# Banded attention, gated projections and an MLP on one core: other PSUM banks for the attention's outputs and its transposes

## The chip, the cores and the metric

The kernel runs on one core of a Trainium2 chip. The metric is the device time of one execution in microseconds (us). Three timed runs of the kernel before gave 503.07, 503.93 and 504.25 us; the median is 503.93 us.

## What is computed

The program is one chain of three layers on two sequences (B = 2) of 768 positions, all in float32. First comes banded attention with eight heads of 64: a position sees the positions less than `n_local` = 96 before it and the first `n_global` = 8, with a linear bias by distance. Second is a gated layer of four experts, each a causal attention of width 64; each position takes the two experts with the highest gate. Third is a low-rank mixing over positions, followed by an MLP of width 2048 (weights arrive as 64-bit floats).

```python
scores = scale * np.matmul(q, k.transpose(0, 1, 3, 2)) + bias      # layer 1, banded
a = np.exp(scores - scores.max(-1)); a = a / (a.sum(-1) + 1e-09)
attn = np.matmul(a, v)
...
ye = softmax(causal((x @ wq[e]) @ (x @ wk[e]).T)) @ (x @ wv[e]) @ wo[e]   # layer 2
out += mask * w * ye
...
u = x + (x.T @ U @ V).T                                           # layer 3
return u + np.maximum(u @ w_ch1, 0.0) @ w_ch2
```

## The kernel before, in words

**Units.** Layer 1 is cut into 48 units (`a_unit`): for each sequence b, four head pairs j, six row blocks i of 128 positions. A unit goes through all engines. TensorE computes the scores into a score bank S (L223). VectorE adds the bias and finds the row minimum (L240), ScalarE takes the exponential (L244), VectorE the reciprocal of the sum (L248, L249), GpSimd scales the rows (L251). TensorE transposes the scaled rows, two or four blocks of 128x128, into one PSUM bank (L185 in `transpose_out`); ScalarE (L189) or, for each fifth unit, VectorE (L191) copies that bank to SBUF as `pt`. At last TensorE multiplies `pt` with the values into the bank X (L260), called the output products here. Three units share one X tile, a third of the columns each. After the third, ScalarE writes the high part of the tile to `xT` (`hi_act`, L62), and VectorE subtracts it from the tile to make the low part (`lo_dve`, L68). Only then can the next tile in the same bank begin.

**Banks.** PSUM has eight banks in this kernel: T, U, X, `acc`, and two pairs for scores, of which one pair is later given to `acd`. `ps(tag)` looks in the dictionary `rot` for a list of banks that a tag uses in turn; a tag that is not there always has its own bank. Before the change the transposes alternate between T and U, and all output tiles lie in X.

**Stages.** `run` names the stages with `go`, which draws yields from generators in proportion. (1) The 24 units of sequence 0 beside 21 of the 24 steps of W' (`W`), which loads the first MLP weight in pieces, narrows it from 64 bits on ScalarE, GpSimd and VectorE (L77, L79, L80, L81), multiplies it by the output projection on TensorE into `acc` (L474) and splits the product on ScalarE and VectorE. Then the rest of W' and the load of the projection weights. (2) The first projections `C(0)` beside the first six units of sequence 1. (3) The causal attention `D` of sequence 0 beside the other 18 units. Later stages hold the second sequence's projections and the MLP.

**Order.** The order of each engine's instructions is fixed when the program is built: a list scheduler takes those whose inputs it holds ready, by their place in the program and by a model of durations. Each engine then works its list in that order. So a change of banks changes which instruction the scheduler holds ready, and may change all five orders. The dense variant (`run(True)`, behind an `If`) uses the same dictionary and is not executed with these inputs.

Of the kernel before, what the change touches and what calls it, by code (L numbers as in the profile page):

```python
# [19 lines left out]
B, H, S, D = 2, 8, 768, 64  # L20
# [6 lines left out]
R = 32  # L27
# [19 lines left out]
class Body:  # L47
# [615 lines left out]
    def run(self, dense):  # L663
        self.cms = {}
        self.last = None
        self.sb = {"pt": 3, "pr": 6}
        self.fl, self.fmod = 0, FA
        self.psb = {"T": 1, "U": 1, "X": 1, "acc": 1, "acd": 2, "h": 2}
        self.psum = self.open("psum", space=PSUM)
        self.psumT = self.open("psumT", space=PSUM)  # L670
        self.psumR = self.open("psumR", space=PSUM)
        self.psumS = self.open("psumS", space=PSUM)
        self.pp = {"U": self.psumT, "S": self.psumS, "R": self.psumR}
        self.rot = {"T": ["T", "U"], "S": ["S", "R"]}
        const = self.open("const")
        self.small = self.open("small")
        wpp = self.open("wpp")
        zp = self.open("zp")
        self.sA = self.open("sA")
        self.consts(const)  # L680
        self.causal(const)
        stk0 = self.open("stk0", "right")
        wpl = self.open("wpl", "right")
        x1p = self.open("x1p", "right")
        x0p = self.open("x0p", "right")
        self.xT = [[x.tile([P, 4, S], F32R, name=self.uid("xT")) for _ in "hl"] for x in (x0p, x1p)]
        ap = self.open("ap")
        if dense:
            for b in range(B):
                self.A_dense(b, ap)  # L690
            gens = [None, None]
        else:
            self.araw = self.open("araw", bufs=2)
            prep = self.a_prep(0, 0, True)
            pre = next(prep)
            bt = self.open("bt")
            self.band_bias(ap, bt)
            self.close(bt)
            next(prep)
            gens = [self.A(0, pre), lambda: self.A(1, self.pre1)]  # L700

        st0 = self.stacks(stk0)
        self.cv = self.open("cv")
        wtmp = self.open("wtmp")
        W = self.W(wpp, wtmp)
        go(self.tc, (gens[0], 24), (W, 19, 0, 21))
        self.wall_load(wpl)
        go(self.tc, (W, 1))
        self.close(wtmp, self.cv)

        A1 = None if dense else gens[1]()
        self.banks("acd")
        go(self.tc, (self.C(0, st0), 14), (A1, 6, 0, 6))
        self.close(x0p)
        self.soft = self.open("soft0", "right")
        zT = [zp.tile([P, 2, S], F32, tag="zT", name=self.uid("zT"))]
        self.banks("R")
        self.fmod = FD
        go(self.tc, (self.D(0, st0, zT[0], "acc"), 12), (A1, 18))
        self.close(self.soft)  # L720
        if not dense:
            self.close(self.araw)
        self.close(ap, self.sA)

        self.banks("acd")
        self.sb["pr"] = 4
        self.soft = self.open("soft")
        s1p = self.open("s1p")
        yp = self.open("yp")
        self.cv = self.open("cv")  # L730
        mp = self.open("mp")
        yT = [[], []]
        st1 = self.stacks(s1p)
        self.uv_load(yp)

        w2p = None
        w2 = self.w2_load(lambda: [
            ((stk0, "qk0"), (stk0, "qk1")), ((mp, "w2z"), (stk0, "v")), ((w2p, "w2a"), (w2p, "w2b")),
            ((w2p, "w2h"), (w2p, "w2l")), ((s1p, "qk0"), (s1p, "qk1")), ((w2p, "w2x"), (w2p, "w2y"))])
        go(self.tc, (self.Y(0, zT[0], yp, yp, yT[0], "X", "T"), 5, PY), (self.C(1, st1), 14), (w2, 5, 0, 5))  # L740
        self.close(x1p, wpl)
        w2p = self.open("w2p", "right")
        self.wo_load(mp)
        zT.append(zp.tile([P, 2, S], F32, tag="zT", name=self.uid("zT")))
        self.rot.update({"T": ["T"], "h": ["U"]})
        self.fmod = FM
        D1 = self.D(1, st1, zT[1], "X")
        self.op = (mp, "o", 2)
        M0 = chain(self.M(0, 0, yT[0][0], mp, w2), self.M(0, 1, yT[0][1], mp))
        Y1 = self.Y(1, zT[1], yp, yp, yT[1], "X", "T")  # L750
        go(self.tc, (D1, 12, PM), (M0, 24, 0, 24))
        go(self.tc, (Y1, 4, PM, 4), (M0, 10))
        self.close(self.psumS)
        self.psumS = self.open("psumS", space=PSUM)
        self.pp["h"] = self.psumS
        self.rot["h"] = ["U", "h", "h"]
        self.op = (self.soft, "pr", 4)
        go(self.tc, (Y1, 1, PM), (self.M(1, 0, yT[1][0], mp), 17))
        go(self.tc, (self.M(1, 1, yT[1][1], mp), 1))
        self.close(w2p, stk0, mp, self.cv, yp, s1p, self.soft, zp, wpp, self.small, const, self.psumS, self.psumR, self.psumT, self.psum)  # L760
# [10 lines left out]
def chain(*gens):  # L771
    for g in gens:
        yield from g
# [4 lines left out]
def go(tc, *gens):  # L778
    live = [[g[0], g[1], 0, *(tuple(g[2:]) + (0, 1 << 30)[len(g) - 2 :])] for g in gens if g[0] is not None]
    while live:  # L780
        live.sort(key=lambda x: x[2] / x[1])
        g = live[0]
        if g[2] >= g[4]:
            live.pop(0)
            continue
        try:
            if g[3]:
                with tc.high_priority(g[3]):
                    next(g[0])
            else:  # L790
                next(g[0])
            g[2] += 1
        except StopIteration:
            live.pop(0)
# [57 lines left out]
```

## Time and profile before

| | us |
|---|---|
| median of three runs | 503.93 |
| lowest, highest | 503.07, 504.25 |
| the profiled execution's own time | 504.68 |
| its span, first to last instruction | 502.9 |
| TensorE busy in the span | 474.5 |

The span is 1.8 us shorter than the execution's own time. Busy time is summed per engine; a matmul's duration overlaps the next one's, so a busy TensorE may still be waiting in small steps. Stages 1 and 2 are the first 128 us or so of the span.

### The profile page before, as it was taken

The page shows a single profiled execution, that of the slowest core. Times are in us where ns is not written, and L with a number is a line of the kernel's source. Part 1 is how long each engine was busy: PE and PEld are TensorE (multiplying, and loading weights), DVE is VectorE, ACT ScalarE, POOL GpSimd, SP SyncE. Part 2 cuts the span into 40 slices and gives each one's busy share as a digit, 9 for nine tenths or more (in the row PEclk, how much of TensorE's full clock was granted, in tenths as well). Part 3 has the DMA queues.
Part 4 walks back from the last instruction along what each step waited for, and adds up shares of the span by engine and source line. Part 5 has one row for each costly group of instructions (what it writes and reads, how often), then busy time and mean ns, then how long its engine had stood idle before and what let it go on. Part 6 is the DMA issues. An engine that isn't in the chain of part 4 may idle for free.

```text
span 502.9 us, 8239 instructions
## 1 busy us (share of the span) xinstructions
PE 474.5 (94%) x2916; PEld 368.0 (73%) x2916; DVE 245.6 (49%) x811; ACT 216.9 (43%) x581; POOL 115.6 (23%) x210
## 2 busy tenths in 40 slices
PE   5789999999899999899999998999999999999995
PEld 3465767798466567797767775878887888888883
DVE  5787877635776775994863236212322211112111
ACT  6667763521778876644553346222212111111111
POOL 4735555410455451211521011100000000000000
PEclk9999999999999999999999999999999999999998
DMA  8854766245021003440210000100000100010002
GB/s 287 290 170 171 241 206 219 88 109 180 1 72 59 1 3 125 151 143 1 84 44 1 1 0 1 45 21 1 0 1 0 65 0 1 0 63 1 0 1 69
DMA packets 17650, 36.68 MB, mean 73 GB/s; under 512 B 2560, under 2 KB 6400, under 8 KB 17600
## 3 DMA queue, kind: packets, MB, share of 16 engines
q1 hardware_dynamic: 15728, 34.49, 21.0%
q10 hardware_dynamic: 1872, 1.58, 0.9%
q8 instruction: 25, 0.41, 0.3%
q14 instruction: 25, 0.20, 0.1%
HBM read 32.91 MB, written 3.15 MB: 72 GB/s over the span
## 4 chain that ended last, share of the span: by engine, by line
PE 72%; DVE 10%; DMA 6%; ACT 5%; issue 4%; POOL 2%; SPq 0%; POOLq 0%; ACTq 0%; DVEq 0%
PE acd L309 17%; PE acc L309 9%; PE acd L310 8%; PE U L309 6%; PE S L223 5%; DMA cr<-in_w_dram 4%; PE acc L310 4%; PE T L185 4%; PE X L260 3%; PE h L309 3%; PE U L310 3%; PE acc L474 3%; PE U L185 2%; PE acc L417 2%; DVE ct L81 2%
## 5 line engine op out<-in xcount | busy, mean ns | idle before, releaser
L309 PE MATMUL acd<-w,hh 128*128 128x512 f32 x256 | 84.0, 404 | 0.7 <-ACT hh L564 0.7
L565 DVE SCALAR_TENSOR_TENSOR hl<-U,hh 128x384 fp32r<-128x384 f32 x43 | 23.9, 556 | 96.0 <-ACT hh L564 93.2
L564 ACT ACTIVATE hh<-U 128x384 fp32r<-128x384 f32 x43 | 21.1, 490 | 83.3 <-PE U L310 55.2
L244 ACT ACTIVATE pr<-e,nm 128x256 f32<-128x256 f32 (+1 forms) x96 | 46.2, 483 | 22.8 <-DVE nm L240 22.6
L251 POOL TENSOR_SCALAR pr<-pr,rec 128x256 f32<-128x256 f32 (+1 forms) x96 | 45.7, 491 | 40.9 <-ACT pr L244 10.1
L309 PEld LDWEIGHTS acd<-w,hh 128*128 128x128 f32 x256 | 46.0, 188 | 12.1 <-ACT hh L564 2.7
L406 POOL TENSOR_SCALAR pm<-pm,rec 128x128 f32<-128x128 f32 (+5 forms) x48 | 32.5, 690 | 93.8 <-DVE rec L404 59.3
L310 PE MATMUL acd<-w,hl 128*128 128x512 f32 x128 | 50.6, 395 | 0.0
L309 PE MATMUL U<-yT,wph 128*128 128x384 f32 x172 | 45.1, 342 | 0.3 <-DVE hl L565 0.3
L223 PE MATMUL S<-kx,qr 64*128 64x256 f32 (+1 forms) x192 | 34.8, 427 | 7.0 <-ACT qr L214 5.9
L309 PE MATMUL acc<-w,hh 128*128 128x512 f32 x128 | 40.6, 395 | 0.0
L399 ACT ACTIVATE pm<-pm,nm 128x128 f32<-128x128 f32 (+5 forms) x48 | 31.7, 662 | 18.9 <-DVE nm L394 18.2
L189 ACT ACTIVATE pt<-T 128x512 f32<-128x512 f32 (+1 forms) x52 | 27.4, 528 | 24.8 <-PE T L185 24.6
L565 DVE SCALAR_TENSOR_TENSOR hl<-h,hh 128x384 fp32r<-128x384 f32 x21 | 11.7, 557 | 52.8 <-ACT hh L564 44.7
L79 POOL TENSOR_SCALAR cr<-cr 128x512 f32<-128x512 f32 (+2 forms) x35 | 24.5, 708 | 45.7 <-ACT ct L77 40.0
L309 PEld LDWEIGHTS U<-yT,wph 128*128 128x128 f32 x172 | 31.4, 188 | 4.2 <-DVE hl L565 0.5
L474 PE MATMUL acc<-ct,woT 128*128 128x256 f32 x128 | 31.4, 386 | 3.2 <-DVE ct L81 2.1
L564 ACT ACTIVATE hh<-h 128x384 fp32r<-128x384 f32 x21 | 10.3, 491 | 52.4 <-PE acd L309 41.1
L80 DVE SCALAR_TENSOR_TENSOR cr<-cr 128x512 int32<-128x512 int32 (+2 forms) x35 | 25.8, 744 | 13.1 <-POOL cr L79 10.9
L240 DVE CUSTOM_DVE_ANT_0 e<-S,dw 128x256 f32<-128x256 f32 x80 | 30.3, 415 | 1.9 <-PE S L223 1.7
L77 ACT ACTIVATE ct<-cr 128x512 f32<-128x512 f32 (+2 forms) x35 | 22.9, 658 | 14.7 <-DMA cr<-in_w_dram 13.3
L310 PE MATMUL U<-yT,wpl 128*128 128x384 f32 x86 | 29.2, 339 | 0.0
(175 smaller groups left out, 961.6 us busy)
## 6 DMA issues: line engine op xcount, KB each, us to landing
cr<-in_w_dram SPq DMA_DIRECT2D x32, 512.0 KB, 4.2
kx<-in_kx_dram SPq DMA_DIRECT2D x7, 464.0 KB, 6.3
v<-in_v_dram SPq DMA_DIRECT2D x8, 384.0 KB, 4.0
qr<-in_q_dram SPq DMA_DIRECT2D x7, 384.0 KB, 5.5
va<-in_va_dram SPq DMA_DIRECT2D x8, 320.0 KB, 4.0
cr<-in_wall_dram SPq DMA_DIRECT2D x4, 386.0 KB, 3.7
out_dram<-o SPq DMA_DIRECT2D x12, 128.0 KB, 1.9
out_dram<-o ACTq DMA_DIRECT2D x12, 128.0 KB, 2.1
```

Source lines behind the costliest of these rows:

```text
L185: nc.tensor.transpose(t[:, n * P : (n + 1) * P], src(n), self.ident)
L223: self.nc.tensor.matmul(sp[:, h, :], q[s], k[s], start=True, stop=True)
L240: nc.vector.tensor_tensor_reduce(out=e[:, h, :w], in0=sp[:, h, :w], in1=bt, scale=-slope(2 * j + h), scalar=HUGE, op0=ALU.add, op1=ALU.min ...
L244: nc.scalar.activation(pr[:, h, :w], e[:, h, :w], AF.Exp, bias=nm[:, h : h + 1], scale=-1.0, accum_out=den[:, h : h + 1])
L251: nc.gpsimd.tensor_scalar(pr[:, h, :w], pr[:, h, :w], rec[:, h : h + 1], 0.0, op0=ALU.mult, op1=ALU.add)
L309: mm(out, lh, rh, start=first, stop=False), mm(out, lh, rl, start=False, stop=False),
L310: mm(out, ll, rh, start=False, stop=last)]
L399: nc.scalar.activation(prs[h][:, :w], prs[h][:, :w], AF.Exp, bias=nm[h], scale=-1.0, accum_out=den[:, h : h + 1])
L406: nc.gpsimd.tensor_scalar(prs[h][:, :w], prs[h][:, :w], rec[:, h : h + 1], 0.0, op0=ALU.mult, op1=ALU.add)
L474: nc.tensor.matmul(ac, woT[:, kc, ps], w1[kc // 2][:, kc % 2, :], start=kc == 0, stop=kc == 3)
L564: nc.scalar.activation(hh, hp, AF.Relu)
L565: nc.vector.scalar_tensor_tensor(hl, hp, 0.0, hh.bitcast(F32), op0=ALU.max, op1=ALU.subtract)
```

## The change

In stages 1 and 2 the output tiles of the banded attention alternate between the banks X and U, and all transposes go to T. From stage 3 on the banks are as before: transposes alternate between T and U, output tiles are in X.

```diff
@@ run
-        self.rot = {"T": ["T", "U"], "S": ["S", "R"]}
+
+        self.rot = {"T": ["T"], "X": ["X", "U"], "S": ["S", "R"]}
@@ run, ahead of the stage with D of sequence 0
         self.banks("R")
         self.fmod = FD
+        self.rot.update({"T": ["T", "U"], "X": ["X"]})
         go(self.tc, (self.D(0, st0, zT[0], "acc"), 12), (A1, 18))
```

## Rows read from the trace of the kernel before

**Rows 1.** The page: busy us of each engine, share of the span, instructions.

```profile
PE 474.5 (94%) x2916; PEld 368.0 (73%) x2916; DVE 245.6 (49%) x811; ACT 216.9 (43%) x581; POOL 115.6 (23%) x210
```

**Rows 2.** Busy time by window of 25 us, from 0 to 100 us.

```profile
core 0: us, PE busy (x) PEld busy (x) DVE busy (x) ACT busy (x) POOL busy (x), PEclk, DMA share, GB/s
0.00:25.00 25.00, 16.02 (x90) 9.51 (x90) 16.20 (x74) 15.49 (x45) 14.40 (x39) 1.00 0.86 290
25.00:50.00 25.00, 22.29 (x163) 15.32 (x161) 19.48 (x72) 17.32 (x55) 11.08 (x23) 1.00 0.52 168
50.00:75.00 25.00, 23.38 (x178) 17.86 (x177) 19.59 (x75) 18.22 (x58) 13.22 (x26) 1.00 0.72 229
75.00:100.00 25.00, 23.77 (x164) 18.66 (x164) 17.51 (x51) 11.86 (x38) 12.17 (x19) 1.00 0.47 155
```

**Rows 3.** Waits of TensorE from 0 to 128 us: total us, times, longest.

```profile
PE X L260 <- DVE xT L68: 2.3, 2, 1.8
PE acc L474 <- DVE ct L81: 2.1, 1, 2.1
PE U L185 <- POOL pr L251: 2.0, 2, 1.2
```

**Rows 4.** Timeline, first change of the X tile: start, duration, engine, instruction, [idle before].

```profile
20.31 0.39 PE L260 MATMUL X<-pt,v 128*64 128x128 f32 x4
...
25.08 0.47 ACT L62 ACTIVATE xT<-X 128x384 fp32r<-128x384 f32 x1
...
26.30 0.54 DVE L68 TENSOR_TENSOR xT<-X,xT 128x384 fp32r<-128x384 f32 x1
...
26.89 0.44 PE L260 MATMUL X<-pt,va 128*64 128x128 f32 x4 [1.80 <-DVE xT L68]
```

**Rows 5.** Timeline, the other change of tile at which TensorE waited.

```profile
59.54 0.44 PE L260 MATMUL X<-pt,va 128*64 128x128 f32 x4 [0.47 <-DVE xT L68]
```

**Rows 6.** Timeline, transposes and copies of units 3 to 6.

```profile
15.59 0.66 PE L185 MATMUL U<-ident,pr 128*128 128x128 f32 x4
...
16.99 0.66 ACT L77 ACTIVATE ct<-cr 128x512 f32<-128x512 f32 x1 [1.43 <-DMA cr<-in_w_dram]
...
18.54 0.57 ACT L189 ACTIVATE pt<-T 128x512 f32<-128x512 f32 x1
...
18.98 1.13 PE L474 MATMUL acc<-ct,woT 128*128 128x256 f32 x4 [2.10 <-DVE ct L81]
...
22.81 0.79 PE L185 MATMUL U<-ident,pr 128*128 128x128 f32 x4
...
26.75 0.68 DVE L191 COPY pt<-T 128x512 f32<-128x512 f32 x1
```

**Rows 7.** Timeline, transposes and copy of units 21 and 22.

```profile
67.42 0.60 PE L185 MATMUL U<-ident,pr 128*128 128x128 f32 x4
...
70.29 0.58 ACT L189 ACTIVATE pt<-T 128x512 f32<-128x512 f32 x1
```

**Rows 8.** Groups by line, 0 to 128 us: copies of transposes, high and low parts.

```profile
L189 ACT ACTIVATE pt<-U 128x512 f32<-128x512 f32 x12 | 7.1, 589 | 1.1 <-PE U L185 1.1
L189 ACT ACTIVATE pt<-T 128x512 f32<-128x512 f32 (+1 forms) x12 | 6.1, 510 | 0.4 <-PE T L185 0.3
...
L62 ACT ACTIVATE xT<-X 128x384 fp32r<-128x384 f32 x10 | 4.8, 478 | 3.9 <-PE X L260 3.9
...
L68 DVE TENSOR_TENSOR xT<-X,xT 128x384 fp32r<-128x384 f32 x10 | 5.5, 548 | 0.6 <-ACT xT L62 0.6
...
L191 DVE COPY pt<-U 128x512 f32<-128x512 f32 x3 | 2.0, 676 | 0.0
L191 DVE COPY pt<-T 128x512 f32<-128x512 f32 (+1 forms) x3 | 1.8, 586 | 0.0
```

**Rows 9.** Timeline, the last transposes of stage 2 and the first of stage 3.

```profile
113.88 0.60 PE L185 MATMUL U<-ident,pr 128*128 128x128 f32 x4
...
129.40 0.33 PE L185 MATMUL T<-ident,pm 128*128 128x128 f32 x1 [0.77 <-POOL pm L406]
```

## The prediction

> **What bounds the kernel now.** I read the page first. TensorE is busy for 474.5 of 502.9 us, and VectorE, next, for about half [rows 1]. The table by windows says where TensorE is not busy. In the first 25 us it lacks 9.0 us; in the next three windows it lacks 2.7, 1.6 and 1.2 us, and the granted clock is 1.00 in each [rows 2]. So the banded stage beside W' is bound by TensorE after its start, with VectorE at 19.5 of 25 us as the nearest second. A change of banks removes no work here; it can pay only by what TensorE idles. The list of its waits names the idle time, and three entries matter: output products waiting for VectorE's low part, 2.3 us in two waits; W' products waiting for a narrowed piece, 2.1 us; transposes waiting for GpSimd, 2.0 us in two [rows 3].
>
> Then I read the timeline around the first entry. The output products of unit 3 end about 20.7 us. The high part of that X tile is written from 25.08, the low part from 26.30 to 26.84, and the next products start at 26.89 after an idle 1.80 us [rows 4]. The X bank was shut for 6.2 us, of which the two reading instructions take 1.0; the rest is their place in the lists of ScalarE and VectorE. The other wait is 0.47 us [rows 5]. In stages 1 and 2 there are ten such changes of tile [rows 8]; at the other eight TensorE had other work at hand, and no wait is shown.
>
> **The change, part by part.** No instruction is added or taken away, and no DMA: 48 units keep their scores, transposes, copies and products. What changes is who waits for which bank, and through it the lists.
>
> (a) Output tiles in X and U in turn. The first products of a group then wait for the reading of the tile two groups back, which is three units earlier and done. Both waits go: 1.80 + 0.47 = 2.27 us, a gain [rows 4, 5]. What is late next: at 26.89 sixteen product instructions ran at once, those of units 4 and 5. Unit 4's `pt` can be read much earlier; unit 5's is copied by VectorE only from 26.75 to 27.43 [rows 6], which keeps part of the late products where they are. The W' products must fill the hole, and these come as their pieces are narrowed.
>
> (b) Transposes in T alone. Unit n+1's transposes now wait for the copy of unit n's. I set starts against the ends of the copies. Unit 4's transposes start at 15.59 while unit 3's copy ends at 18.54 + 0.57 = 19.11: 3.52 us early. Unit 6's start at 22.81, unit 5's copy ends at 27.43: 4.62 us. Unit 22's start at 67.42, unit 21's copy ends at 70.87: 3.45 us [rows 6, 7]. These are the longest among 30; of the others most start after the copy's end or within a microsecond of it. The upper bound of the loss is these three in full, 11.6 us, if every list stays as it is, since all that stands behind a waiting transpose in TensorE's list stands too. The lower bound is nothing: the scheduler knows the wait and puts ready work in front, and VectorE or ScalarE takes the copy earlier. A gain is excluded for this part, since it only adds an order. What covers it is other TensorE work: scores of later units and, from 18.98 on, W' products. Before 18.98 there is none of the latter, and TensorE idles 2.10 us waiting for the first piece [rows 6]. So unit 4's block of four transposes, 0.66 us, moves out of a stretch that ends in idle time into one in which it costs. That is the row it is nearest to, and I take 0.7 us; unit 6's block lands where (a) leaves a hole, and unit 22's where W' products and the next scores are ready: nothing for both. If that cover is gone, 3.5 to 4.6 us each.
>
> (c) ScalarE, VectorE and GpSimd behind it. The copy is the instruction that both orders now wait for. On ScalarE unit 3's copy comes at 18.54, behind a narrowing step that itself waited 1.43 us for its DMA [rows 6]; the scaled rows of the next units stay in their four buffers meanwhile. I put nothing on it in the sum and let it carry the second rival.
>
> (d) The turn back at stage 3. Stage 2's last transposes are at 113.88, stage 3's first at 129.40 [rows 9]. Both T and U have been read by then: nothing, in either direction. Stages 3 and later keep their banks; only the lists' order may differ, which I can't price and put at nothing.
>
> Sum: -2.27 + 0.7 = -1.6 us. The profiled execution took 504.68 us (span 502.9 and 1.8 outside it), 0.75 above the median of the runs. Against its own time the changed kernel comes to 503.1; against the median, 503.93 - 1.6 = **502.3 us**.
>
> One rule weighs against this change. The rows show the transposes handing their bank over 30 times in stages 1 and 2 (24 + 6 copies, 17.0 us together), the output tiles ten times (high and low parts, 10.3 us) [rows 8]: the two banks in turn move from the frequent handover to the rare one. The Trainium skill, Perfetto Trace Analysis, section Optimizing Tensor Performance, says that independent matmul groups should rotate through different PSUM banks so that the reading of one overlaps the matmuls of the next. By that rule both should rotate, and if only one can, the one with more handovers; it gives no price, and what it would make of the time is the third rival below. The waits of TensorE speak the other way so far: none is shown for a copy of transposes in the three entries, while the output tiles have 2.3 us.
>
> **The rivals.** First, *given back*: the waits at X go, and another takes their place, the pieces of W' (2.1 us of waiting [rows 3]) or VectorE, busy 78% there [rows 2]. For it: TensorE lacks only 1.2 to 2.7 us per window, and a product that runs earlier leaves a hole later. Against it: a hole filled early is work done, as long as TensorE bounds the windows to 100 us. The time stays within 1 us of 503.9. That the alternation doesn't happen at all, because a group's tile is set up only when the unit's products are, and the scheduler places them as before, ends at the same time.
>
> Second, *the transposes' bank blocks*: slower. At the start, between 13 and 27 us, ScalarE's list holds copies behind narrowing steps that wait for DMA. If units 4 and 6 wait their 3.52 and 4.62 us in TensorE's list, that is 8.1 us, less the idle time that is there already (2.10 and 1.80), less the 0.47 at 59.54: +3.8 us, so 507.7. It decides from the point at which the added waits exceed 2.3 us in places where TensorE had work. For it: both copies are late by their engine's list, not by the transposes; TensorE executes its list in order. Against it: the scheduler draws up the list anew, and the place already idles.
>
> Third, *the frequent handover costs more throughout*: if each of the 30 handovers showed a fifth of its mean copy (17.0 / 30 = 0.57 us), that is 3.4 us; less 2.27, +1.1 us, 505.0. For it: units come in pairs, two transposes close together, as at 67.42. Against it: from unit 4's transposes to unit 22's it is 18 units in 51.8 us [rows 6, 7], 2.9 us for a unit, against 0.66 for four transposes and 0.57 for a copy, so that one bank is needed for less than half of the time. This is the Trainium skill's rule of the paragraph above, taken as a mechanism; the trace bears it out only in that the copies of neighbouring units overlap the transposes at three places.
>
> **How the numbers follow.** A measurement of this kernel can tell about 0.2%, 1 us, from no change. The forecast, faster by over 1 us: 0.47. Given back or without effect: 0.26. The bank blocks at the start: 0.17. The frequent handover: 0.10. So faster 0.47, same 0.26, slower 0.27. The best end takes the transposes' two waits for GpSimd too, because output products of the next group can now stand in front of them: 2.27 + 2.0 = 4.3 us, 499.6. The upper end takes in the third rival and most of the way to the second: 506.5. Beyond it I leave half of the second rival, below it some chance of a better order of the lists, together 0.2. The forecast's own range is 499.6 to 502.9.
>
> **What would show it.** Right: among TensorE's waits from 0 to 128 us none of output products for the low part; output products in X and U in turn; transposes in T alone, each starting after the previous copy's end; TensorE busy for more than 22.3 us between 25 and 50. Given back: the first item holds, but waits for W' pieces or for GpSimd grow by as much, and stage 3's first transposes stay at 129.4 us [rows 9]. The second and third rival: waits of the form transposes for ScalarE's or VectorE's copy, at the start or evenly through the stage. The prediction is wrong if those transposes stay there and the total still moves: then the later stages' order, which I put at nothing, decides.

## The result, and the profile after

The changed kernel took 509.61 us (median of four runs, 508.47 to 510.28) against 504.09 before: a ratio of 1.008, interval 1.0053 to 1.0107. The interval stands for 2.7 to 5.4 us more, and the medians lie 5.5 us apart; 502.3 was forecast, and 506.5 was the upper end. The profiled execution has a span of 507.8 us, 4.9 more than before.

Where in the span does this arise? The timeline of the changed kernel has the first transposes of stage 3 here:

```profile
133.84 0.33 PE L185 MATMUL T<-ident,pm 128*128 128x128 f32 x1 [0.56 <-POOL pm L406]
```

Before they were at 129.40 [rows 9]. So 4.4 of the 4.9 us are lost ahead of stage 3, in the stages in which the banks differ. The busy times by window, in the columns of [rows 2]:

```profile
0.00:25.00 25.00, 17.89 (x88) 11.25 (x90) 15.97 (x78) 15.44 (x45) 14.62 (x39) 1.00 0.85 288
25.00:50.00 25.00, 21.94 (x150) 14.84 (x148) 18.62 (x69) 15.47 (x45) 11.33 (x20) 1.00 0.63 195
50.00:75.00 25.00, 21.69 (x147) 14.98 (x145) 19.40 (x63) 15.48 (x46) 14.46 (x22) 0.99 0.65 222
75.00:100.00 25.00, 24.83 (x162) 18.59 (x161) 14.21 (x56) 13.59 (x43) 11.51 (x19) 0.94 0.38 108
```

From 25 to 75 us TensorE is busy for 43.6 us where it was 45.7, and it does 297 instructions there where it did 341. Between 75 and 100 us it is busier, but at a granted clock of 0.94. Up to 25 us it is busy for longer than before, 17.9 against 16.0 us, with two instructions fewer; the part on the clock returns to that. Its waits, from 0 to 128 us:

```profile
PE S L223 <- DMA kx<-in_kx_dram: 6.1, 2, 4.5
PE S L223 <- DVE nm L240: 5.3, 5, 1.5
PE acc L309 <- ACT xT L62: 1.4, 1, 1.4
PE acc L474 <- DVE wpl L68: 1.3, 3, 0.8
PE X L260 <- ACT pt L189: 1.1, 2, 0.8
```

The first line is the start of the kernel. The 2.3 us at the output tile are gone, as forecast, and so are the 2.1 and 2.0 us at W' pieces and scaled rows [rows 3]. In their place scores wait for VectorE's bias step, 5.3 us, where it was 0.2. No line says that transposes wait for a copy, though that is the one wait that the change adds. It shows in the timeline instead, in the order of TensorE's list. One round of the changed kernel, units 8 and 9:

```profile
39.78 0.66 PE L185 MATMUL T<-ident,pr 128*128 128x128 f32 x4
40.37 0.70 PE L223 MATMUL S<-kx,qr 64*128 64x256 f32 x4
40.48 0.60 ACT L189 ACTIVATE pt<-T 128x512 f32<-128x512 f32 x1
41.00 1.99 PE L474 MATMUL acc<-ct,woT 128*128 128x256 f32 x8
42.93 0.44 PE L260 MATMUL X<-pt,va 128*64 128x128 f32 x4
43.20 0.39 PE L260 MATMUL X<-pt,v 128*64 128x128 f32 x4
43.52 0.66 PE L185 MATMUL T<-ident,pr 128*128 128x128 f32 x4
...
99.56 0.66 PE L185 MATMUL T<-ident,pr 128*128 128x128 f32 x4
```

A unit's transposes, scores of a later unit, eight W' products while the copy is made, this unit's output products, and only then the next transposes. The kernel goes round in lock-step. The last line is unit 24: (99.56 - 39.78) / 16 = 3.74 us a unit, as the mean of steps between 2.0 and 6.1 us. The kernel before has units 8 and 24 here:

```profile
30.76 0.66 PE L185 MATMUL U<-ident,pr 128*128 128x128 f32 x4
...
74.26 0.60 PE L185 MATMUL U<-ident,pr 128*128 128x128 f32 x4
```

That is (74.26 - 30.76) / 16 = 2.72 us a unit. In the round shown the W' products take 1.99 us where the copy takes 0.60, and TensorE does not wait. So W' ends earlier (its last product starts at 94.5 us instead of 104.9), and unit 24 comes 25 us later. Such a trade costs nothing where each gap is filled, and a longer round is not yet a loss.

**The clock.** In the changed kernel's trace the granted clock is 0.50, the lower of the two levels (1.2 of 2.4 GHz), from 74.6 to 78.0 us, shortly after a wait of 1.55 us that ended at 72.84. W' products alone, kernel before and then after, in the columns TensorE, its weight loads, clock, DMA share and GB/s:

```profile
74.60:78.00 3.40, 1.89 (x8) 1.43 (x8) 1.00 0.18 23
```

```profile
74.60:78.00 3.40, 3.30 (x8) 2.05 (x7) 0.50 0.53 164
```

Eight products take 3.30 us instead of 1.89, some 1.4 us. The start is slower too, though the column of the clock gives 1.00 there. Transposes of units 2 and 3 in the changed kernel:

```profile
12.69 1.12 PE L185 MATMUL T<-ident,pr 128*128 128x128 f32 x4
...
17.20 1.12 PE L185 MATMUL T<-ident,pr 128*128 128x128 f32 x4
```

Four transposes take 0.66 us later in this kernel, and already at 15.59 in the kernel before [rows 6]. They take 1.12 us also at 27.43 in the run with T alone below, where the granted clock is 0.50 (26.5 to 29.5 us). Up to the first transposes of stage 3, and from 11.6 to 20 us, kernel before:

```profile
0.00:129.40 129.40, 113.10 (x762) 85.60 (x763) 85.92 (x322) 71.06 (x215) 54.61 (x111) 1.00 0.59 191
11.60:20.00 8.40, 5.47 (x40) 3.30 (x39) 5.09 (x21) 5.89 (x20) 5.19 (x10) 1.00 0.92 349
```

Changed kernel:

```profile
0.00:133.84 133.84, 116.97 (x762) 86.72 (x763) 84.28 (x322) 73.45 (x215) 59.43 (x111) 0.99 0.57 184
11.60:20.00 8.40, 7.65 (x40) 4.82 (x36) 5.59 (x28) 6.52 (x21) 6.09 (x11) 1.00 0.95 358
```

Both do 762 TensorE instructions ahead of stage 3, and TensorE is idle for 16.3 us before and 16.9 after. So in this one pair of traces 3.9 of the 4.4 us are longer busy time and not longer waiting. That does not make the clock the cause. A stretch at the lower level shows in most of the traces below, and also in one that is no slower (stage 2 alone, with a mean granted clock of 0.93 from 25 to 50 us). Two of the four runs of the changed kernel have a mean granted clock of 0.997 and took 508.47 and 509.62 us; the runs of the kernel before with 0.997 or more, measured beside the experiments, took 502.66 to 504.57. That mean leaves out the slow start; a kernel below has the same start and loses nothing.

### The profile page after: what moved, and what is told of

Its sections match the earlier page's. It is cut to its first block, busy times and chain, and to the rows that moved or that the text cites. A ratio compares the mean times of both kernels' runs of the same rounds, so it can differ in the third digit from the quotient of the medians.

```text
span 507.8 us, 8260 instructions
## 1 busy us (share of the span) xinstructions
PE 478.7 (94%) x2916; PEld 369.5 (73%) x2916; DVE 244.0 (48%) x811; ACT 219.7 (43%) x581; POOL 121.0 (24%) x210
## 4 chain that ended last, share of the span: by engine, by line
PE 75%; DVE 8%; ACT 6%; DMA 4%; issue 3%; POOL 2%; SPq 1%; POOLq 0%; ACTq 0%; DVEq 0%
PE acd L309 17%; PE acc L309 8%; PE acd L310 8%; PE U L309 6%; PE S L223 5%; PE T L185 5%; PE acc L474 4%; PE acc L310 4%; PE h L309 3%; PE U L310 3%; PE X L260 2%; ACT pr L244 2%; DMA qr<-in_q_dram 2%; PE acc L417 2%; PE X L417 2%
## 5 line engine op out<-in xcount | busy, mean ns | idle before, releaser
L251 POOL TENSOR_SCALAR pr<-pr,rec 128x256 f32<-128x256 f32 (+1 forms) x96 | 49.6, 529 | 47.2 <-DVE rec L249 23.7
L564 ACT ACTIVATE hh<-U 128x384 fp32r<-128x384 f32 x43 | 21.1, 490 | 81.9 <-PE U L310 53.9
L189 ACT ACTIVATE pt<-T 128x512 f32<-128x512 f32 (+1 forms) x64 | 34.8, 544 | 37.5 <-PE T L185 37.0
L223 PE MATMUL S<-kx,qr 64*128 64x256 f32 (+1 forms) x192 | 35.3, 447 | 12.5 <-DMA kx<-in_kx_dram 6.1
L474 PE MATMUL acc<-ct,woT 128*128 128x256 f32 x128 | 33.4, 405 | 1.3 <-DVE wpl L68 1.3
L223 PEld LDWEIGHTS S<-kx,qr 64*128 64x128 f32 x192 | 17.8, 210 | 22.9 <-DVE nm L240 8.3
L80 DVE SCALAR_TENSOR_TENSOR cr<-cr 128x512 int32<-128x512 int32 (+2 forms) x35 | 24.1, 690 | 13.9 <-POOL cr L79 11.5
```

What stands on the lines that cost most here:

```text
L189: nc.scalar.activation(pt[:, :w], t[:, :w], AF.Copy)
L223: self.nc.tensor.matmul(sp[:, h, :], q[s], k[s], start=True, stop=True)
L251: nc.gpsimd.tensor_scalar(pr[:, h, :w], pr[:, h, :w], rec[:, h : h + 1], 0.0, op0=ALU.mult, op1=ALU.add)
L474: nc.tensor.matmul(ac, woT[:, kc, ps], w1[kc // 2][:, kc % 2, :], start=kc == 0, stop=kc == 3)
L564: nc.scalar.activation(hh, hp, AF.Relu)
```

## The experiments

The theory (A) was that the single bank of the transposes paces the units; the rivals were that the alternating output tiles put TensorE's list in a worse order (B), or a chance place at which TensorE idled and its clock fell (C).

**One half alone, and one stage alone.** Transposes in T alone, with the output tiles back in X alone:

```diff
-        self.rot = {"T": ["T"], "X": ["X", "U"], "S": ["S", "R"]}
+        self.rot = {"T": ["T"], "X": ["X"], "S": ["S", "R"]}
```

> Stages 1 and 2 with the transposes in T alone and the output tiles in X alone; U is idle there. Theory A (the single bank of the transposes paces the units, and the second bank of the output tiles gives next to nothing): about the changed kernel's time, 509 to 512 us, units' transposes spaced by some 3.7 us in stage 1, scores waiting for VectorE by 4 us or more from 0 to 134 us. Theory B (what costs is the other half, output tiles alternating, which puts output products and W' products in another order): 503 to 505 us. Theory C (nothing of the banks, only a bad place at which TensorE idled and its clock fell): anything from 503 to 507, with unit spacing near 2.9 us.

Measured: 511.38 us, ratio 1.014 (1.010 to 1.0179); 3.65 us a unit. The loss is the transposes' bank, and the second bank of the output tiles has no part in it: B falls, and a chance place (C) does not space 16 units. That it is 1.8 us slower than the changed kernel may be the clock: its runs have a mean granted clock of 0.984 to 0.991, the changed kernel's 0.988 to 0.997. The step back to the old banks was then put ahead of stage 2 (the next run), or the new ones were used in stage 2 only (the run after it):

```diff
+        self.rot.update({"T": ["T", "U"], "X": ["X"]})
         go(self.tc, (self.C(0, st0), 14), (A1, 6, 0, 6))
```

> The changed banks in stage 1 only; the old banks come back ahead of stage 2. Theory A: the lag of TensorE's work arises between 35 and 80 us, in stage 1, so most of the loss stays: 507.5 to 510 us. If stage 2's six units carry the loss (transposes there some 4 to 5 us apart): 503.5 to 506 us.

> The old banks in stage 1, the changed banks in stage 2 only. Theory A: no loss beyond a measurement's reach in stage 1, little in stage 2 because TensorE has the projections to do: 503 to 505 us. If stage 2 carries the loss: 507 to 510 us.

Measured: stage 1 alone 510.45 us, ratio 1.0107 (1.0061 to 1.0153); stage 2 alone 503.74 us, ratio 0.999 (0.9969 to 1.0012). The loss is in stage 1; stage 2 alone shows none.

**Buffers of scaled rows.** Why do scores wait for VectorE? One answer was that late transposes hold the four buffers of scaled rows.

```diff
-        pr = soft.tile([P, 2, 2 * P], F32, tag="pr", name=self.uid("pr"), bufs=4)
+        pr = soft.tile([P, 2, 2 * P], F32, tag="pr", name=self.uid("pr"), bufs=6)
```

> The changed kernel with six buffers of scaled rows in place of four. Theory A says the late transposes hold those buffers, so that the exponentials stop, VectorE's bias step stops behind them, and scores wait for VectorE: with two more buffers the waits of scores for VectorE fall from 5.3 us to under 3, the time to 506 to 508.5 us, while the transposes stay spaced by 3.5 us or more. If the scores wait for VectorE's own list (steps of the narrowing in front of the bias step), the waits stay at 4 us or more and the time at 509 to 511 us.

Measured: 510.84 us, ratio 1.0107 (1.0057 to 1.0156), and these waits of TensorE from 0 to 134 us:

```profile
PE acc L474 <- DVE wpl L68: 3.6, 4, 1.9
PE S L223 <- DVE nm L240: 2.7, 2, 1.4
PE X L260 <- ACT pt L189: 2.4, 3, 1.3
PE U L260 <- ACT pt L189: 1.4, 2, 0.9
```

The waits of the scores fell to 2.7 us, as expected of the theory, and the time did not follow: W' products and output products wait instead. So it does not matter which of TensorE's instructions waits. Transposes stayed 3.7 us apart.

**A third of the handovers.**

```diff
-        self.rot = {"T": ["T"], "X": ["X", "U"], "S": ["S", "R"]}
+        self.rot = {"T": ["T", "T", "U"], "X": ["X"], "S": ["S", "R"]}
```

> Stages 1 and 2 with the transposes in T, T, U in turn and the output tiles in X alone: of three handovers one is in the same bank at once (T to T), two are between banks. If the cost goes by handovers within one bank, a third to a half of the 7 us that T alone costs: 505.5 to 508.5 us. If any single handover in the same bank already makes the lock-step: 509 to 512 us. If nearly none: 503 to 505 us.

Measured: 508.64 us, ratio 1.008 (1.0051 to 1.0109), just above the range for a third to a half of the loss. Units are 2.90 us apart. By the middle values that is more than half of T's 1.4% for a third of its handovers, but the intervals leave room for a third, so it is not shown that the cost is out of proportion. A single wait of 3.4 us (scores for VectorE) and a mean granted clock of 0.86 from 25 to 50 us are part of this run's loss.

**The handover by itself.** W' left out of stage 1, so that nothing fills the gap, once with the old banks and once with the new:

```diff
-        W = self.W(wpp, wtmp)
-        go(self.tc, (gens[0], 24), (W, 19, 0, 21))
+        self.wp = [wpp.tile([P, 2, DFF], F32R, name=f"wp{x}") for x in "hl"]
+        for t in self.wp:
+            nc = self.nc
+            nc.gpsimd.memset(t.bitcast(F32), 0.0)
+        go(self.tc, (gens[0], 24))
         self.wall_load(wpl)
-        go(self.tc, (W, 1))
```

> The kernel before without W' in stage 1: its loads, narrowing and products are left out, and the first MLP weight is zero. This is the base of the next run. The 24 units stand alone; their spacing shows what the units' own chain allows with two banks for the transposes: some 2 us a unit.

> The changed kernel without W' in stage 1, as in the run before this one. If the handover of the single bank is what costs (transposes, copy, the next transposes, with the semaphores between), the units' spacing is longer than with two banks by 0.3 us or more, and the time longer than that run's by 5 us or more. If the loss arises only from how W' products and units mesh, the two runs are within 2 us.

Measured: 475.95 us with the old banks, 497.04 with the new: 21.1 us. Units 8 to 24 are 1.89 and 2.37 us apart. The traces have spans of 474.1 and 496.5 us, and the first transposes of stage 3 here, old banks and then new:

```profile
101.63 0.66 PE L185 MATMUL T<-ident,pm 128*128 128x128 f32 x2
```

```profile
114.43 0.68 PE L185 MATMUL T<-ident,pm 128*128 128x128 f32 x2 [0.63 <-POOL pm L406]
```

So 12.8 of the 22.4 us lie ahead of stage 3, about three times the 4.4 us of the full kernel: W' hid most of it. The other 9.6 us arise where both kernels have the same banks. The clock has a share on either side: in the second kernel the mean granted clock is 0.86 from 25 to 50 and from 100 to 125 us, 0.93 from 125 to 150 and 0.94 from 175 to 200; in the first it is 1.00 in all four. The timeline of the second shows the bare loop:

```profile
43.88 0.66 PE L185 MATMUL T<-ident,pr 128*128 128x128 f32 x4
...
44.57 0.60 ACT L189 ACTIVATE pt<-T 128x512 f32<-128x512 f32 x1 [0.62 <-PE T L185]
...
44.88 0.70 PE L223 MATMUL S<-kx,qr 64*128 64x256 f32 x4 [0.35 <-DVE nm L240]
...
45.52 0.44 PE L260 MATMUL X<-pt,va 128*64 128x128 f32 x4
...
45.78 0.39 PE L260 MATMUL X<-pt,v 128*64 128x128 f32 x4
...
46.10 0.66 PE L185 MATMUL T<-ident,pr 128*128 128x128 f32 x4
```

0.69 us from the transposes to the copy, 0.95 from the copy to the output products, 0.58 for these, then the next transposes: 2.22 us. The copy frees T and completes `pt` at the same moment, and the products, which come first in the program, go first. So the products stand in the loop although they don't use T.

**The products out of the loop.** Each unit's output products written one unit later, behind the next unit's transposes:

```diff
         pt = self.transpose_out(...)
+        self.flush()
+        self.pend = (b, j, i, nk, pt, v, va)
+
+    def flush(self):
+        if self.pend is None:
+            return
...
         if i % 3 == 0:
             self.xp = self.ps("X")
...
```

> The changed kernel with each unit's output products written one unit later, behind the next unit's transposes; nothing else. If the loop that paces the units is transposes, copy, output products, next transposes, the products leave it: spacing falls from 3.7 us towards 3 us, the time to 503 to 507 us. If the loop is transposes and copy alone, or the lists mesh badly for another reason, 508 to 512 us.

> The kernel before with the same deferral: the control. Two banks in turn already let the next transposes go ahead of the copy, so the deferral changes no loop: 502 to 506 us. Were it to gain as much as in the run before this one, the gain would not be that loop's.

> The changed kernel without W' in stage 1 (its loads, narrowing and products are left out, and the first MLP weight is zero), with the deferral. Without the deferral such a kernel spaced its units by about 2.3 us. If the products are in the loop: 1.8 us or less, and 480 to 488 us in place of 497. If not: 2.3 us and 495 to 499 us.

Measured: the changed banks with the deferral 503.47 us, ratio 0.9976 (0.9958 to 0.9995); the old banks with it 504.97 us, ratio 1.0001 (0.9978 to 1.0025); the new banks without W' 484.55 us instead of 497.04. The deferral takes the whole loss off the changed kernel and does nothing for the old one: the loss is that loop. Up to the first transposes of stage 3, with the deferral, changed banks and then old:

```profile
0.00:129.47 129.47, 116.74 (x766) 87.42 (x766) 83.88 (x326) 73.06 (x218) 58.78 (x111) 1.00 0.59 190
```

```profile
0.00:130.76 130.76, 118.57 (x762) 89.36 (x762) 85.08 (x322) 71.94 (x215) 53.91 (x111) 0.96 0.57 189
```

With the changed banks TensorE is busy for as long as without the deferral (116.7 against 117.0 us), and idle for 12.7 us instead of 16.9: nearly all of the 4.4 us by which stage 3 starts earlier is waiting that is gone. The old banks with the deferral are busier still, at a granted clock of 0.96, and idle for 12.2 us. So a slower TensorE can take its time out of the idle time, but in the lock-step it did not: with T alone it is idle for 16.7 us ahead of stage 3, with the new banks in stage 1 alone for 19.5. Why the lock-step keeps its idle time is argued here from one trace of each kernel.

Without W' the deferral gains 12.5 us, but in the traces only 1.0 us of that lies ahead of stage 3, whose first transposes are at 113.41. There the loop shows in the spacing of the units and not in the time. A round of the deferred kernel without W' (lines have moved by the edit: L186 transposes, L190 copy, L270 products, L224 scores):

```profile
61.09 0.63 PE L186 MATMUL T<-ident,pr 128*128 128x128 f32 x4
61.64 0.44 PE L270 MATMUL X<-pt,va 128*64 128x128 f32 x4
61.81 0.60 ACT L190 ACTIVATE pt<-T 128x512 f32<-128x512 f32 x1 [1.31 <-PE T L186]
61.91 0.39 PE L270 MATMUL X<-pt,v 128*64 128x128 f32 x4
62.23 0.70 PE L224 MATMUL S<-kx,qr 64*128 64x256 f32 x4
62.87 0.66 PE L186 MATMUL T<-ident,pr 128*128 128x128 f32 x4
```

The products of the unit before now cover the copy, and this round takes 1.78 us. The mean is 2.05, above the 1.8 that I had expected. With W' the units close up only from 3.74 to 3.33 us, while the whole loss of time is recovered. So spacing alone is not what the time follows: it matters whether TensorE has something to do while the copy runs, and now it can have the products there, whether a W' piece is ready or not.

**The second bank of the output tiles, once the loop is mended.** The deferral, with output tiles in X alone (the same diff as in the first experiment):

> Deferred output products, transposes in T alone, output tiles in X alone (U idle in stages 1 and 2). Against the changed kernel with the deferral, 503.5 us, it lacks only the second bank of the output tiles. If that bank is worth the waits that the prediction took for it, some 2.3 us: 505 to 507 us, with output products waiting for VectorE's low part. If it is worth nothing: 503 to 504.5 us.

Measured: 504.38 us, ratio 0.9993 (0.9974 to 1.0012); output products wait 0.6 us for the low part, once. Against 0.9976 with the second bank that is 0.9 us more, and the intervals overlap: a gain of the second bank isn't shown.

**Priority, a miss.** Stage 1's units put 300 places ahead of W' in the scheduler's order:

```diff
-        go(self.tc, (gens[0], 24), (W, 19, 0, 21))
+        go(self.tc, (gens[0], 24, 300), (W, 19, 0, 21))
```

> The changed kernel with the 24 units of stage 1 put 300 places ahead of W' in the scheduler's order. If the transposes lag only because W' products stand in front of them in TensorE's list, the units close up to some 3 us spacing and the time falls to 504 to 507 us. If each unit's transposes wait for the copy before them in whatever order, and W' products only fill the gap, spacing stays near 3.7 us and the time at 509 to 512 us.

Measured: 516.46 us, ratio 1.0248 (1.0211 to 1.0285), outside both. Units are 3.9 us apart. This run can't separate the two answers, since the list took a form that costs by itself: one unit's transposes and another's products singly in turn.

```profile
78.75 0.43 PE L260 MATMUL U<-pt,va 128*64 128x128 f32 x2 [0.32 <-ACT pt L189]
79.11 0.33 PE L185 MATMUL T<-ident,pr 128*128 128x128 f32 x1
79.37 0.43 PE L260 MATMUL U<-pt,va 128*64 128x128 f32 x2
79.73 0.33 PE L185 MATMUL T<-ident,pr 128*128 128x128 f32 x1
...
81.14 1.89 PE L474 MATMUL acc<-ct,woT 128*128 128x256 f32 x8
```

## Why the prediction was wrong

**Part (b) failed, by its size.** It put 0.7 us on the transposes' bank; T alone costs 1.4%, 7 us (5 to 9), with the clock's share in it. The upper bound, 11.6 us, would have held. Two choices led to the low value. I priced three places at which the old trace had transposes ahead of a copy, and took the nearest row for one of them (a fourth, unit 3 at 13.04, starts 1.9 us ahead of the end of unit 2's copy, and was overlooked); but a bank that is handed over by every unit makes a loop at every unit, in a list that is drawn up anew. And the cover was taken for complete. W' products do fill most of the gaps: ahead of stage 3 the loss is 12.8 us without W' and 4.4 with it. That the rest is gaps at which no W' piece was ready is not shown; what is shown is that the loss goes when the output products stand there.

**The argument against the third rival was wrong.** It said that one bank is needed for less than half of the time, 0.66 us of transposes and 0.57 of copy in 2.9. The loop has more in it: the handover to the other engine and back, and the output products, which the same copy sets free. Bare, it is 2.2 us, not 1.2, of the 2.9 that a unit had. That rival had the right mechanism, and the wrong price (a fifth of a copy per handover). With one bank to give, the transposes need it more (1.014 without it). The Trainium skill, Perfetto Trace Analysis, section Optimizing Tensor Performance, says that independent matmul groups should rotate through banks; the run with T alone agrees, and the runs with the deferral show the same time without such a rotation (0.9993 with T alone and X alone). So the bound that part (b) adds nothing was reachable by order alone.

**Part (a) isn't shown.** Both waits at the output tile are gone, as forecast, but with T alone and X alone no output product waits for the low part from 0 to 134 us either, so the second bank was not needed for that. What the second bank is worth isn't shown: 511.38 without the second bank and 509.61 with it, intervals 1.010 to 1.0179 and 1.0053 to 1.0107, fit the 2.27 us of the sum, but touch; with the loop mended they overlap more.

**The second rival did not decide.** The start has its share of the delay: unit 8's transposes are 9.0 us late already (39.78 against 30.76). But 16 of the 25 us by which unit 24's transposes are late come after unit 8, 1.0 us with each unit. And the changed kernel with the deferral has the same start without the loss: its transposes of units 2 and 3 take 1.11 and 1.09 us, and its unit 8 is 7.2 us late:

```profile
37.91 0.60 PE L186 MATMUL T<-ident,pr 128*128 128x128 f32 x4
```

So a late and slow start alone does not cost the time.

**Parts (c) and (d).** The buffers of scaled rows, put at nothing, show no gain in time (510.84 us with six, 509.61 with four). The turn back at stage 3 costs little if anything: 4.4 us of lag ahead of it, 4.9 at the end.

**The sign to look for** was wrong too: transposes waiting for a copy do not appear among the changed kernel's waits. The scheduler knows of that wait and puts them late in the list, and what the list already holds is seen as spacing.

## What to carry to other kernels

Before giving a bank away, draw the loop that it closes: from one use through the other engine to the next use, with everything that the order of the program puts ahead of the next use. Then count rounds, and ask what TensorE does during each reading. Where two things wait for the same copy, write the one that frees the bank first: here that made one bank as good as two, and 503.47 us (0.9976, 0.9958 to 0.9995) is the lowest ratio of the kernels here that leave nothing out. A gain over the kernel before isn't shown by it: its runs had a granted clock of 0.994 to 0.999, those of the kernel before beside them 0.987 to 0.998.

## What the runs showed of the hardware that was not expected

Transposes (128 rows by 128 columns) and output products (64 columns of the array), singly in turn, took 2.39 us for four transposes and eight product instructions, from 78.75 to 81.14. In blocks, in the changed kernel, eight product instructions and four transposes start at 42.93 and give way to the scores at 44.10: 1.17 us. No experiment looked into the cause.
